# First half of k over SyncE in fp32, loads held until the transposes before them, and a product put behind two copies

## The chip, the core and the metric

The kernel runs on one core of a Trainium2 chip. A core has five engines that work side by side, each through its own instruction queue in order: TensorE for matrix products (PE in the profile; its weight loads are PEld), VectorE (DVE), ScalarE (ACT), GpSimd (POOL) and SyncE (SP). Data moves between the chip's memory and the core's on-chip memory by 16 DMA engines. SyncE, ScalarE and GpSimd can issue DMAs; a DMA that changes the type on the way (fp32 in memory, bf16 on chip) is issued from GpSimd in this kernel. TensorE writes its products to PSUM banks; the other engines take them from there.

The metric is the device time of one execution in microseconds. Before the change it is 317.12 us, the median of three runs (315.88 to 319.26).

## The reference

Attention with pooled keys and values, followed by a feed-forward block with the activation h·cos(h). Batch 8, 8 heads, 576 tokens, head size 64; k and v are averaged over groups of 8 tokens, so that each head attends to 72 pooled positions.

```python
B, H, S, D = q.shape                       # 8, 8, 576, 64, float32
k_p = k.reshape(B, H, S // 8, 8, D).mean(axis=3)
v_p = v.reshape(B, H, S // 8, 8, D).mean(axis=3)
scores = np.matmul(q, k_p.transpose(0, 1, 3, 2)) / np.sqrt(D)
attn = softmax(scores)                     # over the 72 pooled positions
a = np.matmul(attn, v_p)
x = a.transpose(0, 2, 1, 3).reshape(B * S, H * D)     # 4608 tokens x 512
h = x @ w_in                               # 4608 x 2048
out = (h * np.cos(h)) @ w_out              # 4608 x 512
```

## The kernel before

**Tiles and stages.** The 4608 tokens form nine tiles of 512. A tile `t` goes through an up phase and a down phase. In the up phase (`up_mm`, `up_g`), eight steps `fp` each make two 128-column chunks of h by eight matmuls into one of three two-bank buffers `banks[fp % 3]`; ScalarE takes the cosine (line 280), VectorE multiplies into `g_sb` (line 283). In the down phase, 64 matmuls (`down_mm`, line 286) accumulate four blocks of 128 tokens in two alternating buffers `obanks`; VectorE copies each finished block out (`down_out`, line 292) and SyncE stores it (line 296). Since 576 tokens of a batch are more than 512 of a tile, batch `b = t + 1` is being prepared while tile `t` runs, and a rest of 64 tokens of batch `t` is done in tile `t` as well.

**Attention inside the down phase.** A list `fill` holds pairs of a position and a piece of attention work. Before down matmul number `n`, all pieces with a position up to `n` are issued. `scores` (line 198, then an exponential on ScalarE, line 202) and `values` (line 224, then two logarithms, one exponential that forms the inverse, and two products on VectorE that write the next tile's input `xT`, lines 230 to 233) work on four units of a batch, here named `S_(n, bank)` and `V_(n, bank)`. They share the buffers `banks` with one another, so a unit must have left a bank before the next can enter it. In tile 0 the down matmuls run in an order that uses the four quarters of the down weights one after another, for two token blocks at a time: the copies of the first two blocks come after matmuls 27 and 31.

**Pooling k and v, transposing q and k.** Batches 0 and 1 are loaded in a layout with two rows of positions to a partition pair (`load_even`, line 85, GpSimd) and pooled on TensorE (`pool_k_mm`, line 154; `pool_v_mm`, line 162), q is transposed on TensorE (`q_transpose_mm`, lines 189 and 190). From batch 2 on, GpSimd loads k, q and v (lines 104 and 85, from `load_kv` and `load_even`) and pools by additions (`pool_add`, lines 138 to 145), k into `kpz` and v into `vz`. The transposes are then DMAs that SyncE issues in the up phase: q's after step 0 (`q_transpose`, line 181), k's after step 2 (`k_transpose`, line 168), into `qT` and `kz[b % 2]`.

**What orders the work.** The schedule is by hand: each engine takes its instructions in the order in which the program issues them, and waits only for semaphores. GpSimd's order from batch 2 on is loads of k, q, v, then k's additions, then v's, batch after batch; it goes on as soon as buffers are free (two each for `kv_st` and `q_b`), however far TensorE is. SyncE's order is the output stores of a tile, then the next tile's q transpose, then its k transpose. The program's order in a tile with `t > 0` is: up phase with the two transposes of batch `t + 1`, loads of batch `t + 2` (lines 445 to 449), down phase, additions of batch `t + 2` (lines 467 to 469).

**The head.** Ahead of tile 0 lies batch 0 (lines 310 to 398). TensorE runs ten warm-up matmuls, pools the first half of k (heads 0 to 3), runs two more warm-up matmuls, transposes the first half of q, and then computes scores; the second halves follow, then v. GpSimd issues, in this order, the first half of k (line 318), two small index tables, the first half of q (line 327), the second half of k, an identity matrix, the second half of q, v, and then the weights and batch 1. VectorE builds the 0/1 matrix `groups` that pools.

Of the kernel before, what the change touches and what calls it, by code (L numbers as in the profile page):

```python
# [9 lines left out]
FP32 = mybir.dt.float32  # L10
BF16 = mybir.dt.bfloat16
# [8 lines left out]
def kernel(  # L20
# [9 lines left out]
    nc = tc.nc  # L30
    B, H, S, D = q.shape
# [8 lines left out]
    ROW = S // 64  # L40
# [6 lines left out]
    REST = (SEG[2], (0, H))  # L47
# [5 lines left out]
    consts = ctx.enter_context(tc.tile_pool(name="consts", bufs=1))  # L53
# [10 lines left out]
    g_sb = wpool.tile([128, FFCH, TILE], BF16, name="g_sb")  # L64

    SpA = -(-Sp // 16) * 16
    kz = [wpool.tile([128, 2 * H, SpA], BF16, name=f"kz{i}") for i in range(2)]
# [5 lines left out]
    banks = [psum.tile([128, 2, 512], FP32, name=f"bank{i}") for i in range(3)]  # L73
# [5 lines left out]
    staged = {}  # L79

    def even_view(src, b, j0=0, j1=KCH):
        return src[b, 2 * j0:2 * j1].rearrange("(j a) (p t) d -> (a p) j (t d)", a=2, t=ROW)

    def load_even(dst, b, src, j0=0, j1=KCH):
        nc.gpsimd.dma_start(out=dst[:, j0:j1].rearrange("p j t d -> p j (t d)"), in_=even_view(src, b, j0, j1))

    def kv_tile():
        return kvst.tile([128, 2 * H * POOL * D], BF16, name="kv_st", tag="kv_st")
# [9 lines left out]
    def q_tile(b):  # L98
        staged["q", b] = qst.tile([128, KCH, ROW, D], BF16, name="q_b", tag="q_b")

    def load_kv(b, which, src):

        st = kv_tile()[:Sp].rearrange("p (i h t d) -> p i h t d", i=2, h=H, t=POOL)
        nc.gpsimd.dma_start(out=st[:, 0].rearrange("p h t d -> p h (t d)"),  # L104
                            in_=src[b].rearrange("h (p t) d -> p h (t d)", t=POOL))
        staged[which, b] = st

    def load_w_in(cg):
        nc.gpsimd.dma_start(
            out=w_in_sb[cg],  # L110
            in_=moe_w_in[:, cg * 512:(cg + 1) * 512].rearrange("(k p) f -> p k f", p=128))
# [8 lines left out]
    half = (slice(0, 64), slice(64, 128))  # L120
# [10 lines left out]
    def pool_add(b, which):  # L131

        st = staged.pop((which, b))
        x = st[:, 0]
        s = st[:, 1].rearrange("p h t d -> p (h t d)").bitcast(FP32).rearrange(
            "p (h t d) -> p h t d", h=H, t=POOL // 2)
        add = nc.gpsimd.tensor_tensor
        add(out=s, in0=x[:, :, 0:4, :], in1=x[:, :, 4:8, :], op=ADD)  # L138
        add(out=s[:, :, 0:2, :], in0=s[:, :, 0:2, :], in1=s[:, :, 2:4, :], op=ADD)  # L139
        if which == "k":  # L140
            for slot in (0, 3):
                add(out=kpz[b % 2][:Sp, :, slot, :], in0=s[:, :, 0, :], in1=s[:, :, 1, :], op=ADD)  # L142
        else:
            s = s.rearrange("p (j a) t d -> p j a t d", a=2)
            add(out=v_part(b), in0=s[..., 0, :], in1=s[..., 1, :], op=ADD)  # L145
# [12 lines left out]
    def pool_v_mm(b, pair):  # L158
        vb = staged["v", b]
        for t in range(ROW):  # L160
            for hp, rows in enumerate(half):
                nc.tensor.matmul(pair[:Sp, hp, 0:KCH * D], lhsT=groups[rows, t, :], rhs=vb[rows, :, t, :],  # L162
                                 start=(t == 0), stop=(t == ROW - 1))
        nc.vector.tensor_copy(out=v_part(b).rearrange("p j a d -> p a j d"),
                              in_=pair[:Sp, :, 0:KCH * D].rearrange("p a (j d) -> p a j d", j=KCH))
# [39 lines left out]
    def x_out(b, u, rows):  # L205
        (c0, n), (h0, nh) = u
        return xT[rows, h0 // 2:(h0 + nh) // 2, b * S + c0:b * S + c0 + n]

    def cols(x, u):
        n = u[0][1]  # L210
        return x[:, 0:n * u[1][1] // 2].rearrange("p (j n) -> p j n", n=n)
# [3 lines left out]
        inv = asb.tile([128, 512], FP32, name="inv", tag="inv", bufs=3)  # L215
        return lnc[:, 0:w], inv[:, 0:w]

    def values(b, u, pair):

        (c0, n), (h0, nh) = u  # L220
        ex = att.pop(("ex", b, u))
        for i in range(nh):
            pj, hp = divmod(h0 + i, 2)
            nc.tensor.matmul(pair[:, hp, (i // 2) * n:(i // 2 + 1) * n],  # L224
                             lhsT=vz[b % 2][:, pj, 2 * hp:2 * hp + 2, :].rearrange("p a d -> p (a d)"),
                             rhs=ex[:, i * n:(i + 1) * n])
        w = nh * n // 2
        lnc, inv = inverse_tile(w)
        for hp in range(2):
            nc.scalar.activation(out=lnc[half[1 - hp]], in_=pair[half[1 - hp], hp, 0:w], func=ACTF.Ln)  # L230
        nc.scalar.activation(out=inv, in_=lnc, func=ACTF.Exp, scale=-1.0)  # L231
        for hp in range(2):
            nc.vector.tensor_mul(out=x_out(b, u, half[hp]), in0=cols(pair[half[hp], hp, :], u),  # L233
                                 in1=cols(inv[half[1 - hp]], u))

    def sums_first(b, u, cs):

# [77 lines left out]

    kv_even_tiles(0)
    q_tile(0)
    load_even(staged["k", 0], 0, k, 0, 2)

    row_of = consts.tile([128, ROW], FP32, name="row_of")  # L320
    for rows in half:
# [2 lines left out]
    first_of = consts.tile([128, Sp], FP32, name="first_of")  # L324
    nc.gpsimd.iota(first_of, pattern=[[POOL, Sp]], base=0, channel_multiplier=0,
                   allow_small_or_imprecise_dtypes=True)
    load_even(staged["q", 0], 0, q, 0, 2)
    load_even(staged["k", 0], 0, k, 2, 4)
    identity = consts.tile([128, 128], BF16, name="identity")
    make_identity(nc, identity)  # L330
# [6 lines left out]
                            in1=first_of.unsqueeze(1).to_broadcast([128, ROW, Sp]), op=mybir.AluOpType.subtract)  # L337
# [3 lines left out]
    nc.vector.memset(vz[0], float(POOL))  # L341
    ones = consts.tile([128, D], BF16, name="ones")
    nc.vector.memset(ones, float(POOL))
    half_pi = consts.tile([128, 1], FP32, name="half_pi")
    nc.vector.memset(half_pi, math.pi / 2.0)

# [21 lines left out]
    us = BY_HEADS  # L368
# [31 lines left out]
    for t in range(NT):  # L400
        b = t + 1
        for fp in range(FFCH // 2):
            up_mm(t, fp, 2 if t == 0 and fp < 2 else 0)
            between = ()
            if t == 0:
                if fp == 4:
                    puts = pool_k_mm(1, obanks[0], 0, 2), pool_k_mm(1, obanks[1], 2, 4)
                elif fp in (5, 6):
                    g0 = 9 * (fp - 5)
                    puts = q_transpose_mm(1, obanks[0], g0, g0 + 5), q_transpose_mm(1, obanks[1], g0 + 5, g0 + 9)  # L410
                if fp in (4, 5, 6):
                    puts[0](vec)
                    between = ((puts[1], act),)
            up_g(t, fp, between)
            if 0 < t and b < B:
                if fp == 0:
                    q_transpose(b)
                elif fp == 2:
                    k_transpose(b)
        mms = [(ms, fc) for ms in range(4) for fc in range(FFCH)]  # L420
        if t == 0:
            mms = [(ms, fc) for hm in range(2) for cg in range(4) for ms in range(2 * hm, 2 * hm + 2)
                   for fc in range(4 * cg, 4 * cg + 4)]


        def S_(n, bank):
            return lambda: scores(b, us[n], banks[bank])

        def V_(n, bank):
            return lambda: values(b, us[n], banks[bank])  # L430

        fill = []
        if t < B:
            exp_tables()
            fill = [(1, lambda: scores(t, REST, banks[2])), (12, lambda: values(t, REST, banks[1]))]
        if t == 0:
            fill[1:] = [(2, S_(0, 0)), (4, lambda: pool_v_mm(1, banks[1])), (8, lambda: values(t, REST, banks[2])),
                        (8, S_(1, 0)), (8, V_(0, 1)), (14, S_(2, 2)), (16, V_(1, 0)), (22, S_(3, 1)), (32, V_(2, 2)),
                        (40, V_(3, 0))]
        elif b < B:  # L440
            us = BY_TOKENS
            fill[1:1] = [(5, S_(0, 0))]
            fill += [(15, S_(1, 2)), (18, V_(0, 0)), (25, S_(2, 2)), (28, V_(1, 1)), (35, S_(3, 2)), (38, V_(2, 0)),
                     (46, V_(3, 1))]
        if 0 < t and b + 1 < B:
            load_kv(b + 1, "k", k)
            q_tile(b + 1)
            load_even(staged["q", b + 1], b + 1, q)
            load_kv(b + 1, "v", v)
        fi = 0  # L450
        if t == NT - 1:
            mms = mms[:-FFCH]
        for n, (ms, fc) in enumerate(mms):
            while fi < len(fill) and fill[fi][0] <= n:
                fill[fi][1]()
                fi += 1
            down_mm(obanks[ms % 2], ms, fc)
            if fc == FFCH - 1:
                down_out(t, ms, obanks[ms % 2])
        if t < B:  # L460
            sin_tables()
        if t == 0:
            load_kv(2, "k", k)
            q_tile(2)
            load_even(staged["q", 2], 2, q)
            load_kv(2, "v", v)
        if b + 1 < B:
            pool_add(b + 1, "k")
            pool_add(b + 1, "v")
    last_chunk()  # L470
# [28 lines left out]
```

## Time and profile before

| What | us |
|---|---|
| median of three runs | 317.12 |
| the profiled execution | 318.08 |
| its span, first to last instruction | 316.3 |
| PE busy | 297.4 |
| ACT busy | 205.7 |
| DVE busy | 173.3 |
| POOL busy | 130.9 |
| mean granted clock of TensorE | 0.984 of full |

The profile is of one execution. Busy time is summed by engine; an engine that is idle and not the bottleneck costs nothing. PE's 94% of the span says that most of the kernel is bound by TensorE; what can be changed without changing the matmuls is the remainder, where PE waits or runs at a reduced clock. A row of the timeline gives start, length, engine, line, operation, what is written from what, the number of merged instructions, and in brackets the idle time before it with what ended it. SPq rows are instructions of SyncE's queue, and their length is the time until the queue goes on, not until the data has landed. The granted clock is TensorE's, 1.00 being full speed.

### The profile page before, as it was taken

Reading aid. Unit: us, or ns where it says so; the run is one execution under the profiler, and the core shown is the slowest. Engines: PE = TensorE matmul, PEld = TensorE weight load, DVE = VectorE, ACT = ScalarE, POOL = GpSimd, SP = SyncE. Lnnn points to the kernel's source line nnn. Section 1 sums busy time; section 2 is a strip of 40 time slices with the busy share of each in tenths; the row PEclk is TensorE's granted clock in tenths of the full one; section 3 lists DMA queues with packets and bytes.
Section 4 is the critical chain, followed back from the end, with each engine's and each line's share of the span. In section 5 each row is a group of like instructions: output and inputs, shape, how many; then the busy total and the mean of one; then the engine's idle time right before and its main releaser. Section 6 shows DMA issues by size and latency. Waiting matters only on the chain.

```text
span 316.3 us, 4555 instructions
## 1 busy us (share of the span) xinstructions
PE 297.4 (94%) x1766; PEld 154.0 (49%) x1798; DVE 173.3 (55%) x213; ACT 205.7 (65%) x254; POOL 130.9 (41%) x88
## 2 busy tenths in 40 slices
PE   7789899999999299999999999999999999999995
PEld 2555554445544155445544554455445544444444
DVE  6358635565656315575557555755575557515721
ACT  1587787369956359569956995699569956705500
POOL 8572018955982991993298329810000000000000
PEclk9799999999999879999999999999999999999999
DMA  6999998399349909960997099602470230041023
GB/s 91 195 207 207 206 205 166 83 157 161 74 68 183 158 2 151 221 103 3 152 212 108 1 157 217 101 2 48 101 101 0 51 85 0 2 99 33 0 62 74
DMA packets 47847, 33.60 MB, mean 106 GB/s; under 512 B 25937, under 2 KB 43345, under 8 KB 47825
## 3 DMA queue, kind: packets, MB, share of 16 engines
q0 software_dynamic: 20016, 18.36, 37.6%
q1 hardware_dynamic: 27648, 14.82, 24.1%
q8 instruction: 14, 0.23, 0.3%
q10 hardware_dynamic: 160, 0.13, 0.2%
q14 instruction: 9, 0.07, 0.1%
HBM read 36.70 MB, written 9.44 MB: 146 GB/s over the span
## 4 chain that ended last, share of the span: by engine, by line
PE 65%; DMA 15%; POOL 11%; ACT 2%; issue 1%; DVE 1%; POOLq 0%; ACTq 0%; DVEq 0%
PE obank L286 29%; PE bank L273 28%; DMA kv_st<-in_k_dram 12%; POOL kv_st L138 6%; PE bank L224 3%; PE bank L198 3%; POOL kv_st L139 3%; DMA kz<-kpz 2%; POOL kpz L142 2%; PE bank L304 1%; ACT ex L202 1%; ACT L261 0%; ACT cos L280 0%; PE obank L256 0%; POOL vz L145 0%
## 5 line engine op out<-in xcount | busy, mean ns | idle before, releaser
L286 PE MATMUL obank<-w_out_sb,g_sb 128*128 128x512 bf16 x542 | 133.1, 382 | 1.1 <-DVE o_sb L292 0.3
L273 PE MATMUL bank<-xT,w_in_sb 128*128 128x512 bf16 x563 | 125.5, 379 | 0.6
L280 ACT ACTIVATE cos<-bank,half_pi 128x1024 f32<-128x1024 f32 x72 | 80.2, 1115 | 67.3 <-PE bank L273 63.7
L283 DVE TENSOR_TENSOR g_sb<-bank,cos 128x1024 bf16<-128x1024 f32 x72 | 88.1, 1224 | 50.2 <-ACT cos L280 50.2
L273 PEld LDWEIGHTS <-w_in_sb 128*128 128x128 bf16 x576 | 56.1, 98 | 67.3 <-issue 0.4
L286 PEld LDWEIGHTS <-g_sb 128*128 128x128 bf16 x560 | 54.1, 98 | 52.1 <-issue 2.0
L233 DVE TENSOR_TENSOR xT<-bank,inv 64x512 bf16<-64x512 f32 (+1 forms) x72 | 45.3, 630 | 61.0 <-ACT inv L231 57.6
L138 POOL TENSOR_TENSOR kv_st<-kv_st 72x2048 f32<-72x2048 bf16 x12 | 48.8, 4064 | 39.7 <-DMA kv_st<-in_k_dram 39.7
L230 ACT ACTIVATE lnc<-bank 64x512 f32<-64x512 f32 (+1 forms) x72 | 39.2, 544 | 9.2 <-PE bank L224 7.3
L202 ACT ACTIVATE ex<-bank 72x1024 bf16<-72x1024 f32 (+1 forms) x40 | 36.2, 925 | 7.0 <-PE bank L198 6.9
L292 DVE COPY o_sb<-obank 128x512 f32<-128x512 f32 x35 | 23.5, 689 | 15.4 <-PE obank L286 14.8
L198 PE MATMUL bank<-qT,kz 128*72 128x256 bf16 (+1 forms) x192 | 23.8, 257 | 7.3 <-DMA kz<-kpz 6.4
L139 POOL TENSOR_TENSOR kv_st<-kv_st 72x1024 f32<-72x1024 f32 x12 | 28.2, 2347 | 1.0
L198 PEld LDWEIGHTS <-kz 128*72 128x72 bf16 x192 | 18.0, 119 | 16.5 <-DMA kz<-kpz 6.8
L231 ACT ACTIVATE inv<-lnc 128x512 f32<-128x512 f32 (+1 forms) x36 | 21.0, 582 | 1.1
L224 PE MATMUL bank<-ex,vz 72*128 72x256 bf16 (+1 forms) x176 | 20.1, 244 | 0.3 <-ACT ex L202 0.2
L224 PEld LDWEIGHTS <-vz 72*128 72x128 bf16 x176 | 14.0, 98 | 9.7 <-issue 1.1
L142 POOL TENSOR_TENSOR kpz<-kv_st 72x512 bf16<-72x512 f32 x12 | 15.0, 1267 | 0.5
L145 POOL TENSOR_TENSOR vz<-kv_st 72x512 bf16<-72x512 f32 x6 | 7.6, 1265 | 18.1 <-PE bank L224 17.9
L261 ACT ACT_TABLE_LOAD x9 | 11.5, 1283 | 0.9 <-PEq L483 0.7
L264 ACT ACT_TABLE_LOAD x9 | 11.5, 1283 | 0.2
L104 POOL DMA_DIRECT2D kv_st<-in_v_dram x6 | 5.0, 842 | 10.2 <-PE bank L162 10.2
(55 smaller groups left out, 86.8 us busy)
## 6 DMA issues: line engine op xcount, KB each, us to landing
out_dram<-o_sb SPq DMA_DIRECT2D x70, 128.0 KB, 2.5
kv_st<-in_v_dram POOLq DMA_DIRECT2D x8, 576.0 KB, 14.6
kv_st<-in_k_dram POOLq DMA_DIRECT2D x7, 576.0 KB, 9.0
q_b<-in_q_dram POOLq DMA_DIRECT2D x6, 576.0 KB, 11.5
w_in_sb<-in_moe_w_in_dram POOLq DMA_DIRECT2D x4, 512.0 KB, 13.7
w_out_sb<-in_moe_w_out_dram POOLq DMA_DIRECT2D x4, 512.0 KB, 18.3
q_b<-in_q_dram POOLq DMA_DIRECT2D x4, 288.0 KB, 12.2
kv_st<-in_k_dram POOLq DMA_DIRECT2D x2, 288.0 KB, 5.5
```

Source lines behind the costliest of these rows:

```text
L138: add(out=s, in0=x[:, :, 0:4, :], in1=x[:, :, 4:8, :], op=ADD)
L139: add(out=s[:, :, 0:2, :], in0=s[:, :, 0:2, :], in1=s[:, :, 2:4, :], op=ADD)
L198: nc.tensor.matmul(flat[:Sp, i * n:(i + 1) * n].rearrange("p (g n) -> p g n", n=64), lhsT=kz[b % 2][:, 2 * (h0 + i) + r, 0:Sp], rhs=att["q ...
L202: nc.scalar.activation(out=ex[:, 0:nh * n], in_=flat[:Sp, 0:nh * n], func=ACTF.Exp, scale=scale / POOL)
L224: nc.tensor.matmul(pair[:, hp, (i // 2) * n:(i // 2 + 1) * n], lhsT=vz[b % 2][:, pj, 2 * hp:2 * hp + 2, :].rearrange("p a d -> p (a d)"), ...
L230: nc.scalar.activation(out=lnc[half[1 - hp]], in_=pair[half[1 - hp], hp, 0:w], func=ACTF.Ln)
L233: nc.vector.tensor_mul(out=x_out(b, u, half[hp]), in0=cols(pair[half[hp], hp, :], u), in1=cols(inv[half[1 - hp]], u))
L273: nc.tensor.matmul(h[:, j, :], lhsT=w_in_sb[fc // 4][:, ki, (fc % 4) * 128:(fc % 4 + 1) * 128], rhs=xT[:, ki, t * TILE:(t + 1) * TILE], st ...
L280: nc.scalar.activation(out=cos, in_=h, func=ACTF.Sin, bias=half_pi[:, :1])
L283: nc.vector.tensor_mul(out=g_sb[:, 2 * fp:2 * fp + 2, :], in0=h, in1=cos)
L286: nc.tensor.matmul(o, lhsT=g_sb[:, fc, ms * 128:(ms + 1) * 128], rhs=w_out_sb[fc // 4][:, fc % 4, :], start=(fc == 0), stop=(fc == FFCH - 1))
L292: nc.vector.tensor_copy(out=o[:, 0:n], in_=ps)
```

## The change

Four edits, which the diff shows in this order.

The first half of k for batch 0 is no longer loaded and cast by a GpSimd DMA. SyncE loads it as fp32 into `g_sb`, which is free until tile 0 writes it, and ScalarE copies it to bf16 in k's tile. The first half of q takes the place of k as GpSimd's first load; it had stood behind the two index tables.

In tile 0 the pieces of attention work get other positions in the list `fill`. The pooling of v for batch 1 moves from 4 to 8, the second scores from 8 to 11, the first values from 8 to 13, the third scores from 14 to 18, the second values from 16 to 21, the fourth scores from 22 to 26.

The product that ends the second values is not issued with them but at position 32, that is, behind the copies of the first two output blocks on VectorE.

In tiles 1 to 5 the loads of batch `t + 2` move in the program from before the down phase to behind it, and a copy of one element of `kz[b % 2]` by GpSimd goes ahead of them. `kz[b % 2]` is written by the k transpose of batch `b = t + 1`, so GpSimd waits for that transpose before it issues the loads. In tile 0 the loads stay where they were and have no such copy.

```diff
+    def load_q(b):
+        q_tile(b)
+        load_even(staged["q", b], b, q)
+
...
-    def values(b, u, pair):
+    def values(b, u, pair, later=None):
...
         nc.scalar.activation(out=inv, in_=lnc, func=ACTF.Exp, scale=-1.0)
-        for hp in range(2):
-            nc.vector.tensor_mul(out=x_out(b, u, half[hp]), in0=cols(pair[half[hp], hp, :], u),
-                                 in1=cols(inv[half[1 - hp]], u))
+
+        def mul():
+            for hp in range(2):
+                nc.vector.tensor_mul(out=x_out(b, u, half[hp]), in0=cols(pair[half[hp], hp, :], u),
+                                     in1=cols(inv[half[1 - hp]], u))
+
+        if later is None:
+            mul()
+        else:
+            later.append(mul)
...
     kv_even_tiles(0)
     q_tile(0)
-    load_even(staged["k", 0], 0, k, 0, 2)
+    k_first = g_sb.rearrange("p f n -> p (f n)").bitcast(FP32)[:, 0:2 * ROW * D]
+    nc.sync.dma_start(out=k_first.rearrange("p (j n) -> p j n", j=2), in_=even_view(k, 0, 0, 2))
+    nc.scalar.copy(out=staged["k", 0][:, 0:2].rearrange("p j t d -> p (j t d)"), in_=k_first)
+    load_even(staged["q", 0], 0, q, 0, 2)
...
-    load_even(staged["q", 0], 0, q, 0, 2)
     load_even(staged["k", 0], 0, k, 2, 4)
...
+    gate = consts.tile([1, 1], BF16, name="gate")
...
-        def V_(n, bank):
-            return lambda: values(b, us[n], banks[bank])
+        later = []
+
+        def V_(n, bank, wait=None):
+            return lambda: values(b, us[n], banks[bank], wait)
...
         if t == 0:
-            fill[1:] = [(2, S_(0, 0)), (4, lambda: pool_v_mm(1, banks[1])), (8, lambda: values(t, REST, banks[2])),
-                        (8, S_(1, 0)), (8, V_(0, 1)), (14, S_(2, 2)), (16, V_(1, 0)), (22, S_(3, 1)), (32, V_(2, 2)),
-                        (40, V_(3, 0))]
+            fill[1:] = [(2, S_(0, 0)), (8, lambda: pool_v_mm(1, banks[1])), (8, lambda: values(t, REST, banks[2])),
+                        (11, S_(1, 0)), (13, V_(0, 1)), (18, S_(2, 2)), (21, V_(1, 0, later)), (26, S_(3, 1)),
+                        (32, lambda: later.pop()()), (32, V_(2, 2)), (40, V_(3, 0))]
...
-        if 0 < t and b + 1 < B:
-            load_kv(b + 1, "k", k)
-            q_tile(b + 1)
-            load_even(staged["q", b + 1], b + 1, q)
-            load_kv(b + 1, "v", v)
...
-        if t == 0:
-            load_kv(2, "k", k)
-            q_tile(2)
-            load_even(staged["q", 2], 2, q)
-            load_kv(2, "v", v)
+        if 0 < t and b + 1 < B:
+
+            nc.gpsimd.tensor_copy(out=gate, in_=kz[b % 2][0:1, 0, 0:1])
         if b + 1 < B:
+            load_kv(b + 1, "k", k)
+            load_q(b + 1)
+            load_kv(b + 1, "v", v)
             pool_add(b + 1, "k")
             pool_add(b + 1, "v")
```

## The prediction

> **What bounds the kernel now.** I read the windows first, with one window for each token tile (from the first up-projection matmul of the tile to that of the next), then the waits by engine, then the timeline of the tiles that stand out. The window rows give start:end and length, then busy us (instructions) of PE, PEld, DVE, ACT and POOL, the granted clock, the DMA share and GB/s.
>
> ```profile
> span 316.3 us, 4555 instructions
> 20.10:57.72 37.62, 35.47 (x281) 19.26 (x286) 22.21 (x30) 28.07 (x39) 15.47 (x13) 1.00 1.07 185
> 57.72:89.36 31.64, 31.48 (x174) 16.35 (x176) 18.57 (x23) 24.19 (x30) 24.63 (x12) 1.00 0.69 119
> 89.36:129.52 40.16, 33.59 (x174) 16.98 (x177) 18.83 (x23) 24.48 (x30) 26.46 (x16) 0.92 0.85 127
> 129.52:161.33 31.81, 31.65 (x175) 16.45 (x177) 18.99 (x23) 24.14 (x30) 19.65 (x12) 1.00 0.69 120
> 224.62:256.27 31.65, 31.44 (x173) 16.36 (x176) 18.82 (x23) 24.19 (x30) 0.00 (x0) 1.00 0.36 63
> ```
>
> Tiles 1 and 3 to 6 take 31.64 to 31.81 us (the first and last of the last four are shown), with PE busy nearly throughout: TensorE bounds them, and nothing in the change lowers its work. Three stretches stand out: the 20.1 us before tile 0, tile 0 with 37.62 us, and tile 2, which does the same work as tile 1 in 40.16 us at a mean clock of 0.92. Tile 2 therefore loses 40.16 - 31.65 = 8.5 us. Its timeline says why:
>
> ```profile
> 64.33 1.36 SPq L168 DMA_TRANSPOSE kz<-kpz  x1
> 65.27 0.86 POOL L104 DMA_DIRECT2D kv_st<-in_k_dram  x1
> 74.35 4.06 POOL L138 TENSOR_TENSOR kv_st<-kv_st 72x2048 f32<-72x2048 bf16 x1 [6.61 <-DMA kv_st<-in_k_dram]
> 80.91 2.49 POOL L142 TENSOR_TENSOR kpz<-kv_st 72x512 bf16<-72x512 f32 x2
> 91.15 0.84 POOL L104 DMA_DIRECT2D kv_st<-in_k_dram  x1
> 92.31 10.76 SPq L181 DMA_TRANSPOSE qT<-q_b  x1
> 103.16 5.37 SPq L168 DMA_TRANSPOSE kz<-kpz  x1
> 103.67 1.03 PE L286 MATMUL obank<-w_out_sb,g_sb 128*128 128x512 bf16 x4
> 111.05 1.07 PE L198 MATMUL bank<-qT,kz 128*72 128x256 bf16 x4 [6.35 <-DMA kz<-kpz]
> 132.41 3.18 SPq L181 DMA_TRANSPOSE qT<-q_b  x1
> ```
>
> GpSimd runs ahead of PE here. It starts the loads of batch 4 at 91.15, and 1.2 us later SyncE issues the q transpose of batch 3, which shares the DMA engines with the loads of a whole batch. The issue alone takes 10.76 us where the same instruction takes 3.18 us in tile 3. SyncE works in order, so the k transpose gets out only at 103.16, although its source was complete at 80.91 + 2.49 = 83.4, and PE waits 6.35 us for it.
>
> ```profile
> DMA to landing us min/median/max: 4.9/5.5/17.8
> kz<-kpz SPq DMA_TRANSPOSE x6, 3.9
> 112.00:114.00 2.00, 2.00 (x6) 0.66 (x5) 0.00 (x0) 1.02 (x1) 1.92 (x2) 0.50 0.03 8
> ```
>
> The first row belongs to the q transposes (line 181): 5.5 us to landing is usual, and this one is the 17.8. The last row shows the aftermath: the granted clock is 0.50 after the wait, so the matmuls that follow run at half speed. 6.35 us of wait and some 2.1 us of half clock make up the 8.5.
>
> **The gate and the later loads: -8.5 us.** For tiles 1 to 5 GpSimd first copies one element of kz, which k's DMA transpose writes, and only then issues loads for the next batch. Nothing else stands between on GpSimd's queue, so the three load issues and six additions pass no other instruction; they are queued behind the new wait, and SyncE's next transposes wait for them in turn. The copy itself is one element, five times, while GpSimd would idle anyway: nothing, and 0.1 to 0.3 us each if it were busy.
>
> In tile 1 the gate opens when kz of batch 2 has landed, 64.33 + 3.9 = 68.2, where loads went out at 65.27: 3 us later at most. By then no transpose is in flight until the next tile, so tile 2 finds the queues empty. Its q transpose goes out some 3 us after the tile's start (132.41 against 129.52 in tile 3), the k transpose 3.2 us after that, and kz lands 3.9 us later, about 10 us into the tile. Scores need it after the 64 up matmuls, five down matmuls and the last scores of the batch before, in tile 2 at 103.67 + 1.03 - 89.36 = 15.3 us. That leaves 5 us of slack, as in tiles 3 to 6, so I take the whole 8.5.
>
> The opposite cost is that the loads start later. From 65.27 to 74.35 k takes 9.1 us, and the additions to 83.4 another 9.0. A gate at 10.3 us of a tile gives kpz at 28.4; it is wanted at 31.65 + 6.2 = 37.8 in the next tile. So 9 us are to spare, and the cover fails only if the load and additions take 27 us instead of 18. I keep 0 for its cost, with the bounds 0 and the price in the rival below.
>
> **The head: -2.4 us.** Windows of 1 us, then the timeline:
>
> ```profile
> 1.00:2.00 1.00, 0.53 (x2) 0.26 (x3) 0.92 (x2) 1.00 (x1) 0.73 (x1) 1.00 0.00 0
> 1.27 0.87 POOL L85 DMA_DIRECT2D kv_st<-in_k_dram  x1 [0.82 <-POOLq L483]
> 2.79 0.76 POOL L85 DMA_DIRECT2D q_b<-in_q_dram  x1
> 5.85 0.77 PE L154 MATMUL obank<-groups,kv_st 64*64 64x72 bf16 x36
> 6.55 0.61 PE L365 MATMUL bank<-warm 128*128 128x512 bf16 x2
> 6.67 1.28 DVE L129 CAST kz<-obank 64x144 bf16<-64x144 f32 x4 [0.30 <-PE obank L154]
> 9.01 0.51 PE L189 MATMUL bank<-identity,q_b 128*128 128x128 bf16 x5 [1.85 <-DMA q_b<-in_q_dram]
> 11.70 1.93 ACT L202 ACTIVATE ex<-bank 72x1024 bf16<-72x1024 f32 x2 [1.12 <-PE bank L198]
> 20.21 0.63 ACT L247 ACTIVATE inv<-lnc 128x512 f32<-128x512 f32 x1
> 10.00:12.50 2.50, 2.33 (x11) 1.53 (x12) 0.06 (x1) 1.38 (x2) 1.12 (x2) 0.50 1.20 195
> out_dram<-o_sb SPq DMA_DIRECT2D x70, 128.0 KB, 2.5
> L280 ACT ACTIVATE cos<-bank,half_pi 128x1024 f32<-128x1024 f32 x72 | 80.2, 1115 | 67.3 <-PE bank L273 63.7
> ```
>
> k's first half is used at 5.85, when PE's opening warm-up ends as well, so an earlier k alone is worth nothing. In fp32 over SyncE it takes between 2.5 us (the 128 KB stores of that queue) and 4.6 us (GpSimd's load, 1.27 to 5.85), then a ScalarE copy of 128x1152, estimated from the 128x1024 row at 1.115 x 1152/1024 = 1.25 us. SyncE's first issue has no row; with 1.0 us, k is there at 4.8 to 6.9. I take the middle, 5.8, because the payload is nearest to GpSimd's load but the DMA engines are idle then (share 0.00): no change, ends -0.1 and +1.0.
>
> The gain is q's. Its half is issued at 1.27 in place of 2.79. It lands between 1.27 + 4.6 = 5.9 (as k did alone) and 1.27 + 6.2 = 7.5 (its present 2.79 to 9.01, behind another load); I take 6.6, since k still shares the engines, from another queue. PE has its warm-up done at 7.16, so the wait of 1.85 us goes. What is late next is the first copy of qT: five transposes take 0.51 us, to 7.67, and DVE is at its kz casts until 7.95; the second copy is on ScalarE, which is free, and the scores need both. So this is -1.9. The clock was 0.50 after that wait, from 10.0 to 12.5. PE works at that rate for most of the 1.7 us up to the first exponential at 11.70; at full rate I estimate another -0.5. From the first exponential at 11.70 to the last inverse at 20.84 ScalarE is nearly gapless, so the head moves as a block: -2.4, with ends -0.5 (late k) and -2.8.
>
> On the cause of that drop, the Trainium skill ("TensorE: Matmul & The Clock Gate", Part 1) says that the clock halves after an idle window of about 3.4 us. The 1.85 us here are shorter, so the trace does not agree in the head; by the rule the -0.5 would not come and the head would give -1.9.
>
> The other moves here are later issues on GpSimd, each earlier by the 0.8 us of the issue that left its queue. They feed a DMA stream that is full through most of tile 0 (the first row below). With the bf16 half of k no longer in it (128 x 1152 x 2 bytes = 295 KB), it runs ahead by 295 KB at 204 GB/s = 1.4 us.
>
> **Tile 0: -1.6 us.** The rate just used, the waits inside tile 0, and the loads of the down weights:
>
> ```profile
> 42.00:44.00 2.00, 1.76 (x12) 0.99 (x11) 0.84 (x2) 1.95 (x4) 0.00 (x0) 1.00 1.26 204
> 38.97 1.17 PE L162 MATMUL bank<-kv_st,groups 64*72 64x256 bf16 x18 [0.89 <-DVE g_sb L283]
> 43.54 0.63 PE L198 MATMUL bank<-qT,kz 128*72 128x256 bf16 x4 [0.24 <-ACT ex L202]
> 46.86 0.63 PE L198 MATMUL bank<-qT,kz 128*72 128x256 bf16 x4 [0.53 <-DVE xT L233]
> 50.37 1.89 PE L286 MATMUL obank<-w_out_sb,g_sb 128*128 128x512 bf16 x8 [0.29 <-DVE o_sb L292]
> 48.21 1.39 DVE L233 TENSOR_TENSOR xT<-bank,inv 64x512 bf16<-64x512 f32 x2 [1.40 <-ACT inv L231]
> L114 POOL DMA_DIRECT2D w_out_sb<-in_moe_w_out_dram x4: 740/744/757, 15.0 to 25.5; - x4
> DMA to landing us min/median/max: 17.0/18.3/18.6
> ```
>
> These four waits sum to 1.95 us. The new list puts four more down matmuls ahead of v's pooling (0.9 us, the first wait), three ahead of the second scores, and more between each scores and its values. The product at 48.21 stands ahead of the two output copies today and makes PE wait 0.29 for obank; behind them it does not. Played through by these durations, the order leaves about 0.15 for bank 1, 0.1 where the last scores meet the second product, and 0.15 where the last values meet the delayed one: 0.4 remain, so -1.6 (ends 0 and -1.95). All of this rides on the down weights: the last quarter lands about 25.5 + 18.3 = 43.8 today, 42.4 with the stream 1.4 ahead. It is wanted at down matmul 24, about 45.6 - 2.4 = 43.2, and the second quarter has some 0.4 us of margin by the same sum. The load of v for batch 2 waits for the pooling of v, which now ends at the same 40.1, less 2.4: no cost.
>
> **Sum.** -8.5 - 2.4 - 1.6 = -12.5 us. The profiled execution took 318.08 us (its span and 1.8 us around it), giving 305.6. It stands 0.96 above the median of 317.12, and from the median the sum is 304.6; I take 305.2.
>
> **Rivals.** *The head gains only issue time.* If the two first halves share the engines so that q lands hardly sooner, only the 0.8 us taken from GpSimd's queue comes: 318.08 - 8.5 - 1.6 - 0.8 = 307.2. For it: the DMA engines are full by 10.0 us (share 1.20), and k's load is on them together with q's. Against it: they stand idle before 2 us, time that SyncE's load can use. The Trainium skill ("DMA: Bandwidth & Descriptors", Issuing engines are not separate DMA queues) states this rule, that issuing from several engines saves only the issue time; the idle window above shows no engine saturated there.
>
> *The transposes stay slow.* If something other than loads, say the output stores ahead on SyncE, stretched the q transpose, tile 2 keeps its loss: 318.08 - 4.0 = 314.1. Against it: tile 3 has the same stores and needs 3.18 us.
>
> *The gate becomes the bound (slower).* Each load chain then runs from kz to kz: load, additions 9.0, transposes 3.2 + 3.9. With a load of 15.5 us it equals a tile of 31.65; above that every tile waits. The longest load of this line took 21.1 us:
>
> ```profile
> DMA to landing us min/median/max: 8.7/13.7/21.1
> ```
>
> The five gated batches would then add 5 x 5.6 = 28 us: 318.08 - 12.5 + 28 = 333.6. Against it: that load stood behind a full queue in tile 0; at 65.27 one took 9.1.
>
> **Chances.** Forecast 0.73, head by issue time 0.15, transposes slow 0.07, gate as bound 0.05. The range, 302.8 to 310.0, holds the first two with the bounds of head (late k, +1.9) and tile 0 (+1.6), and the median's 1 us below. About 1% (3.2 us) is what a measurement of this kernel can tell from no change. The third case lies at that edge, so: faster 0.90, within 0.05, slower 0.05.
>
> **What would show it.** Tile 2 at 31.7 us with a clock of 1.00 and a q transpose issue near 3 us; each k load issued just after kz lands; no wait of PE on q_b near 7 us and the first exponential near 9.3; tile 0 at 36 us with no wait on o_sb. I am wrong if a wait for kz or qT stands in tiles 3 to 6, if PE waits for w_out_sb in tile 0, or if k's cast ends after 7.

## The result, and the profile after

The kernel after takes 305.48 us, the median of four runs (305.23 to 305.81), against 317.5 us for the kernel before in the same comparison (315.88 to 319.26): a ratio of 0.9621 with a 95% interval of 0.9568 to 0.9675. The profiled execution took 305.34 us, with a span of 303.6. Single executions of the kernel before lie some microseconds apart, those of the kernel after within 0.6 us; what that has to do with the change is part of the experiments. The ratios leave out runs that are over 1.5% above the fastest of their kernel, which also show a lower granted clock.

The windows by tile, in the columns of the prediction (start:end and length, busy time of PE, PEld, DVE, ACT and POOL, clock, DMA share, GB/s):

```profile
17.63:53.56 35.93, 35.74 (x287) 19.34 (x286) 22.30 (x30) 28.18 (x39) 13.93 (x10) 1.00 1.17 203
53.56:85.21 31.65, 31.65 (x178) 16.35 (x177) 18.59 (x23) 24.19 (x30) 26.07 (x16) 1.00 0.65 121
85.21:116.86 31.65, 31.65 (x178) 16.33 (x177) 18.83 (x23) 24.19 (x30) 20.98 (x12) 1.00 0.64 119
```

Between the two profiled executions the spans differ by 316.3 - 303.6 = 12.7 us, and three places hold all of it: the head 20.10 - 17.63 = 2.5, tile 0 37.62 - 35.93 = 1.7, tile 2 40.16 - 31.65 = 8.5. In tile 2 PE is busy for all of its 31.65 us. The timeline of tile 2 shows the new order of SyncE and GpSimd, with PE's scores at the end:

```profile
88.14 2.00 SPq L185 DMA_TRANSPOSE qT<-q_b  x1
90.23 1.39 SPq L172 DMA_TRANSPOSE kz<-kpz  x1
93.86 0.18 POOL L475 COPY gate<-kz 1x1 bf16<-1x1 bf16 x1 [4.98 <-DMA kz<-kpz]
94.10 0.85 POOL L104 DMA_DIRECT2D kv_st<-in_k_dram  x1
100.37 0.60 PE L202 MATMUL bank<-qT,kz 128*72 128x256 bf16 x4
```

The q transpose is issued in 2.00 us where it took 10.76. The gate opens 8.65 us into the tile, the loads follow, and the scores come at 100.37 without a wait: kz is there 6.5 us ahead of them. The gate costs GpSimd waiting, as the sum of its waits says (25.9 us over four of them, the longest 7.4), but nobody pays for it: tiles 1 to 6 all take 31.64 or 31.65 us, and PE waits for kz in none of them.

```profile
POOL gate L475 <- DMA kz<-kpz: 25.9, 4, 7.4
```

In the head, the fp32 load by SyncE, its cast, and what PE and ScalarE do next:

```profile
4.22 1.15 ACT L331 CAST kv_st<-g_sb 128x1152 bf16<-128x1152 f32 x1 [2.19 <-DMA g_sb<-in_k_dram]
7.64 0.45 PE L193 MATMUL bank<-identity,q_b 128*128 128x128 bf16 x5 [0.90 <-DMA q_b<-in_q_dram]
9.41 1.93 ACT L206 ACTIVATE ex<-bank 72x1024 bf16<-72x1024 f32 x2 [0.47 <-PE bank L202]
47.52 4.06 POOL L142 TENSOR_TENSOR kv_st<-kv_st 72x2048 f32<-72x2048 bf16 x1 [8.71 <-DMA kv_st<-in_k_dram]
```

k's cast ends at 5.37. q's transposes still wait 0.90 us, to 7.64, and the first exponential begins at 9.41 in place of 11.70. The last row is GpSimd's first addition on the k of batch 2; it starts when that load has landed, and the load stands at the end of the first, full DMA stream.

### The profile page after: what moved, and what is told of

Its sections match the earlier page's. It is cut to its first block, busy times and chain, and to the rows that moved or that the text cites. A ratio compares the mean times of both kernels' runs of the same rounds, so it can differ in the third digit from the quotient of the medians.

```text
span 303.6 us, 4590 instructions
## 1 busy us (share of the span) xinstructions
PE 295.3 (97%) x1798; PEld 152.5 (50%) x1798; DVE 173.3 (57%) x213; ACT 206.6 (68%) x255; POOL 131.8 (43%) x92
## 4 chain that ended last, share of the span: by engine, by line
PE 85%; DMA 9%; POOL 3%; ACT 1%; issue 0%; DVE 0%; POOLq 0%; ACTq 0%
PE obank L297 38%; PE bank L284 36%; DMA w_out_sb<-in_moe_w_out_dram 6%; PE bank L228 5%; PE bank L202 4%; DMA w_in_sb<-in_moe_w_in_dram 3%; PE bank L315 1%; POOL kpz L372 1%; POOL kv_st L85 1%; POOL q_b L85 1%; ACT L272 0%; ACT cos L291 0%; POOL identity masks.py:199 0%; ACT ex L206 0%; DVE o_sb L303 0%
## 5 line engine op out<-in xcount | busy, mean ns | idle before, releaser
L202 PE MATMUL bank<-qT,kz 128*72 128x256 bf16 (+1 forms) x192 | 22.7, 248 | 0.3 <-ACT qT L194 0.2
L475 POOL COPY gate<-kz 1x1 bf16<-1x1 bf16 x5 | 0.9, 180 | 25.9 <-DMA kz<-kpz 25.9
L85 POOL DMA_DIRECT2D q_b<-in_q_dram x10 | 7.7, 773 | 2.9 <-DMA w_in_sb<-in_moe_w_in_dram 1.4
```

What stands on the lines that cost most here:

```text
L202: nc.tensor.matmul(flat[:Sp, i * n:(i + 1) * n].rearrange("p (g n) -> p g n", n=64), lhsT=kz[b % 2][:, 2 * (h0 + i) + r, 0:Sp], rhs=att["q ...
```

## The experiments

Each kernel is the kernel after with the edit shown, except e1, which is the kernel before with one. e1 to e4 share one chip and its runs of the kernel before, e5 to e8 the next, e9 to e12 the last.

**e1: the gate alone, in the kernel before.**

```diff
+        if 0 < t and b + 1 < B:
+            nc.gpsimd.tensor_copy(out=gate, in_=kz[b % 2][0:1, 0, 0:1])
         if b + 1 < B:
+            load_kv(b + 1, "k", k)      # and q, v; gone from ahead of the down phase
```

> The kernel before with the gate alone: loads of batch t + 2 behind the down phase and behind the copy of kz; head and tile 0 as before. Theory (the gate removes the meeting of loads and transposes in tile 2, 8.5 us): tile 2 in 31.7 us, q transpose issue near 2 to 3 us, time 308.0 to 309.5. Rival (something else slows the transposes, and the gain came from the shift of the head and tile 0): tile 2 stays above 36 us, time above 313.

Measured: 310.02 us (307.61 to 312.06), ratio to the kernel before 0.9771 (0.9681 to 0.9861). Against a difference of 2% the times alone leave it unclear. In the windows of the profiled execution (307.61 us), tile 0 is as before and tile 2 is whole:

```profile
18.14:55.75 37.61, 35.89 (x285) 19.26 (x285) 22.20 (x30) 27.96 (x38) 16.10 (x12) 1.00 1.13 195
87.40:119.05 31.65, 31.65 (x178) 16.35 (x177) 18.82 (x23) 24.18 (x30) 19.53 (x12) 1.00 0.64 119
```

The tile says plainly which theory holds: with the old head and the old tile 0, the gate alone makes tile 2 31.65 us instead of 40.16, which is 8.5 us. The times say less. The four runs fall into two pairs, 307.61 and 308.16 at a mean clock of 0.998 or more, 311.88 and 312.06 at 0.989. The median, 0.5 above the expected range, lies in the gap between them. Where the slower pair lost its clock is not shown, since neither run has a profile.

**e2: everything but the gate.**

```diff
-        if 0 < t and b + 1 < B:
-            nc.gpsimd.tensor_copy(out=gate, in_=kz[b % 2][0:1, 0, 0:1])
```

> The kernel after without the copy that gates the loads; all else as after. GpSimd then issues the loads of batch 4 when the additions for batch 3 end, near 88.9 us, and the q transpose of batch 3 goes out near 88.1. Theory A (what counts is whether load packets are in the queues while the transposes move): q's transpose gets out just ahead of the loads, k's meets them and lands near 98, wanted at 100.3: time 305.5 to 307. Theory B (without the gate the loads meet the transposes in tile 2 as before): a wait of 6 us on kz and half clock after it, time 313 to 314.5.

Measured: 313.46 and 314.47 us in the two runs that the ratio counts, 0.9874 of the kernel before (0.9786 to 0.9962, unclear against 2%); the other two took 321.3 us. The two counted runs lie 8.5 us above the 305.48 of the kernel after, so what the gate is worth is gone, and both lie where theory B put them. The timeline of tile 2 (profiled execution, 314.47 us):

```profile
88.38 2.78 SPq L185 DMA_TRANSPOSE qT<-q_b  x1
88.66 0.84 POOL L104 DMA_DIRECT2D kv_st<-in_k_dram  x1
91.25 5.01 SPq L172 DMA_TRANSPOSE kz<-kpz  x1
106.61 1.07 PE L202 MATMUL bank<-qT,kz 128*72 128x256 bf16 x4 [5.84 <-DMA kz<-kpz]
```

Theory A falls. The q transpose did go out ahead of the loads, by 0.28 us, and its issue took only 2.78 us; but the k transpose met the loads (5.01 us to issue), and PE waits 5.84 us. A head start of 0.28 us protects nothing here, where a q transpose usually takes 5.6 us to land. The place of the loads in the program does nothing either: without the copy they are in the same program order as in the kernel after. It is the wait that holds them. Theory B holds; what the two runs at 321.3 us met besides is not shown by any profile here.

**e3 and e6: the old head.** The same kernel on two chips; e5 is the kernel after beside e6.

```diff
-    nc.sync.dma_start(out=k_first.rearrange("p (j n) -> p j n", j=2), in_=even_view(k, 0, 0, 2))
-    nc.scalar.copy(out=staged["k", 0][:, 0:2].rearrange("p j t d -> p (j t d)"), in_=k_first)
-    load_even(staged["q", 0], 0, q, 0, 2)
+    load_even(staged["k", 0], 0, k, 0, 2)
...
+    load_even(staged["q", 0], 0, q, 0, 2)     # behind the two index tables, as before
```

> The kernel after with the head as before: first half of k by GpSimd first, first half of q behind the index tables. Theory: the head was worth 2.4 us (1.9 of waiting, 0.5 of clock), so 307.9, with the granted clock at 0.50 over 10.0 to 12.5 and the first exponential at 11.7. Rival (only the issue time of 0.8 us counts): 306.3.

> The kernel after once more, on the same chip as the three that follow, as their yardstick: 305.2 to 305.8.

> The kernel after with the head as before, again, for its spread: 305.85 to 311.57 in four runs, with mean granted clocks of 1.00, 1.00, 0.987 and 0.983. Theory (q's first half lands at a time that varies, and a PE idle for over a microsecond so early falls to half clock): again a spread of 3 us or more, each slow time with a clock below 0.99; median 307 to 309. Rival (the spread came from elsewhere on that chip): all within 1 us.

Measured: e3 305.85, 306.35 and 308.8 us in the three runs that the ratio counts, and 311.57 in a fourth; e5 305.30 (304.73 to 305.88), e6 306.15 (305.92 to 307.27). The middle one of e3's three runs is at the rival's 306.3. On the chip where e5 and e6 ran side by side the new head is worth 0.85 us, not 2.4. The timeline of e6:

```profile
7.95 0.45 PE L193 MATMUL bank<-identity,q_b 128*128 128x128 bf16 x5 [0.28 <-DMA q_b<-in_q_dram]
9.71 1.93 ACT L206 ACTIVATE ex<-bank 72x1024 bf16<-72x1024 f32 x2 [0.47 <-PE bank L202]
18.25 6.02 PE L284 MATMUL bank<-xT,w_in_sb 128*128 128x512 bf16 x26
```

With the old order q was there at 7.95, not at 9.01 as in the profiled execution before, the first exponential starts at 9.71, and tile 0 at 18.25. In the profiles of e3 and e1 the old order has q at 7.41 and 8.04. The same order of loads thus delivers q at times 1.6 us apart. And q is not all that tile 0 waits for, as e3 shows:

```profile
7.41 0.45 PE L193 MATMUL bank<-identity,q_b 128*128 128x128 bf16 x5 [0.73 <-DMA q_b<-in_q_dram]
14.37 1.17 PE L166 MATMUL bank<-kv_st,groups 64*72 64x256 bf16 x18 [0.79 <-DMA kv_st<-in_v_dram]
18.25 6.02 PE L284 MATMUL bank<-xT,w_in_sb 128*128 128x512 bf16 x27
```

Here q comes 0.23 us earlier than in the kernel after, whose transposes start at 7.64, and still tile 0 starts 0.62 us later than its 17.63, because PE waits 0.79 us for v. The spread that e6 was to repeat came back as 1.35 us only, with clocks of 0.997 and above, so its first theory, too, holds in part only: q's time varies, but how often it is late differed between the two calls.

**e7: the old head with more warm-up.**

```diff
-    warm_up(2, banks[1][:, 0, :])      # between pooling k and transposing q
+    warm_up(9, banks[1][:, 0, :])
```

> The same with nine warm-up matmuls in place of two between the pooling of k's first half and the transposes of q's, so that PE works until q is there (about 1.5 us more of them). They compute nothing that is used. Theory (the half clock is the larger part of what a late q costs): clocks 0.995 or above in every run, all runs within 1.5 us, median 306.3 to 307. Rival (the cost is the wait for q itself, or a later DMA): the spread of e6 stays.

Measured: 306.51 us (306.31 to 309.0). Five of the six runs lie within 0.65 us, but the one at 309.0 had a clock of 0.994, which the theory excluded; it has no profile. Since e6 beside it had little spread to remove, this run decides nothing; e9 and e10 put the late q there on purpose.

**e9 and e10: q late, without and with warm-up.** Both have the old head; k's second half is loaded ahead of q's first.

```diff
-    load_even(staged["q", 0], 0, q, 0, 2)
     load_even(staged["k", 0], 0, k, 2, 4)
+    load_even(staged["q", 0], 0, q, 0, 2)
...
-    warm_up(2, banks[1][:, 0, :])      # e10 only
+    warm_up(12, banks[1][:, 0, :])
```

> The kernel after with the old head, and q's first half moved behind k's second half on GpSimd, so that q lands about 1.5 us later than in e6 (9 to 9.5 in place of 7.4 to 8.0). Theory (a late q costs its wait and, once PE has been idle for some 2 us this early, a spell of half clock): clock 0.990 or less in most runs, time 308.5 to 312. Rival (a late q costs its wait alone): 307 to 308, clock 1.00.

> The same with twelve warm-up matmuls in place of two ahead of the transposes of q, so that PE is busy until q lands. Theory: the clock stays at 0.995 or above and the time at 307 to 308, that is, the wait alone. Rival (the idle PE has nothing to do with the clock): as e9.

Measured: e9 308.16 us (307.95 to 308.43), e10 307.31 (307.10 to 307.56). The timeline and a window of e9:

```profile
9.38 0.45 PE L193 MATMUL bank<-identity,q_b 128*128 128x128 bf16 x5 [1.95 <-DMA q_b<-in_q_dram]
10.73 1.91 PE L202 MATMUL bank<-qT,kz 128*72 128x256 bf16 x8
10.00:12.50 2.50, 2.28 (x11) 1.50 (x9) 0.36 (x1) 1.25 (x2) 1.38 (x2) 0.50 1.17 182
```

and the same of e10:

```profile
9.87 0.45 PE L193 MATMUL bank<-identity,q_b 128*128 128x128 bf16 x5 [0.93 <-DMA q_b<-in_q_dram]
10.91 1.13 PE L202 MATMUL bank<-qT,kz 128*72 128x256 bf16 x8
10.00:12.50 2.50, 2.50 (x51) 1.90 (x51) 0.49 (x1) 1.45 (x2) 0.97 (x2) 1.00 1.18 189
```

e9 is the head of the profiled execution before, made on purpose: a wait of 1.95 us, half clock over 10.0 to 12.5, and eight score matmuls in 1.91 us. In e10, q comes even later, at 9.87, yet PE's idle time is 0.93 us, the clock stays at 1.00 and the same eight matmuls take 1.13 us; the kernel is 0.85 us faster than e9. The whole-run clocks agree in all four runs of each, 0.992 to 0.994 in e9 and 0.998 to 1.00 in e10, though e9 stops short of the figures of its theory (0.990 or less, 308.5 us or more). So the half clock that the prediction set for a late q is real, and filling most of the wait with matmuls removes it, at 0.85 us. For the wait alone there is only 307.31 - 306.15 = 1.2 us between e10 and e6, from two chips, which is no more than a hint.

**e4 and e11: the old positions, and the new ones without the delayed product.** e4 has the list of the kernel before. e11:

```diff
-                        (11, S_(1, 0)), (13, V_(0, 1)), (18, S_(2, 2)), (21, V_(1, 0, later)), (26, S_(3, 1)),
-                        (32, lambda: later.pop()()), (32, V_(2, 2)), (40, V_(3, 0))]
+                        (11, S_(1, 0)), (13, V_(0, 1)), (18, S_(2, 2)), (21, V_(1, 0)), (26, S_(3, 1)),
+                        (32, V_(2, 2)), (40, V_(3, 0))]
```

> The kernel after with the old positions of the attention pieces in tile 0 and no delayed product. Theory: the order was worth 1.6 to 1.7 us, by waits of PE for bank 1, the exponential, the product and the output copy: 307.1, tile 0 in 37.6 us. Rival (tile 0 is held by the arrival of the down weights, so the order gives little): 305.5 to 306.

> The kernel after with the product issued with its values, ahead of the two output copies; the other new positions stay. Theory: the product at position 21 is then done before the copies are due, because its inverse is ready about 46.3 us and the copy of block 0 only waits for the rest of the product: at most 0.3 us of PE waiting, 305.3 to 305.7. Rival (the delayed product is what the new order rests on): 306 or more.

Measured: e4 306.98 us (306.82 to 307.13), 1.5 above the 305.48 of the kernel after; e11 306.35 (306.20 to 306.48), 0.9 above it; the three stem from different comparisons. In the profiles tile 0 takes 37.61 us in e4 (from 17.60 to 55.21), 36.80 in e11 (from 17.88 to 54.68) and 35.93 in the kernel after. The timeline of e11:

```profile
45.17 1.39 DVE L239 TENSOR_TENSOR xT<-bank,inv 64x512 bf16<-64x512 f32 x2 [1.40 <-ACT inv L235]
46.59 1.29 DVE L303 COPY o_sb<-obank 128x512 f32<-128x512 f32 x2
47.34 1.89 PE L297 MATMUL obank<-w_out_sb,g_sb 128*128 128x512 bf16 x8 [1.15 <-DVE o_sb L303]
```

My theory for e11 falls, and its rival holds. VectorE starts the product at 45.17, since its inverse is ready only then, and is at it until 46.56; block 0 is finished meanwhile, its copy starts at 46.59, and PE waits 1.15 us for the buffer. In the kernel after no such wait is left:

```profile
43.80 0.63 PE L202 MATMUL bank<-qT,kz 128*72 128x256 bf16 x4
46.00 1.89 PE L297 MATMUL obank<-w_out_sb,g_sb 128*128 128x512 bf16 x8
44.90 0.69 DVE L303 COPY o_sb<-obank 128x512 f32<-128x512 f32 x1 [1.15 <-PE obank L297]
46.48 1.39 DVE L239 TENSOR_TENSOR xT<-bank,inv 64x512 bf16<-64x512 f32 x2
```

Of the 1.7 us that the edit takes from tile 0, 0.9 hang on the delayed product: by themselves the new positions bring the output copies nearer to the product and give 0.8.

**e12: the loads late.**

```diff
+            for _ in range(8):
+                nc.gpsimd.memset(idle, 0.0)      # behind the gate, ahead of the loads
```

> The kernel after with eight fills of an unused tile by GpSimd (1.8 us each, 14.3 us in all) between the gate and the loads. They compute nothing that is used. The rival in which the gate becomes the bound, made real: GpSimd's own loop is then 14.3 + 0.3 gate + 7.6 load + 9.0 + 7.7 additions = 39 us against a tile of 31.65. Theory (9 us of slack at most, counted to k's transpose; 7 us counted over GpSimd's whole loop): tiles 1 and 2 still 31.65 us, tiles 3 to 6 longer by 6 to 9 us each, total 328 to 342. Rival (loads have all the time of a tile): 305 to 307.

Measured: 344.39 us, one run. Two of the gates, one row of the fills, the waits of PE for kz in sum, the first of them, and one more wait of PE, in the head:

```profile
104.92 0.18 POOL L476 COPY gate<-kz 1x1 bf16<-1x1 bf16 x1
105.04 14.80 POOL L478 MEMSET idle<- 80x2048 bf16 x8
145.04 0.18 POOL L476 COPY gate<-kz 1x1 bf16<-1x1 bf16 x1
PE bank L202 <- DMA kz<-kpz: 26.7, 4, 7.4
140.76 1.07 PE L202 MATMUL bank<-qT,kz 128*72 128x256 bf16 x4 [7.39 <-DMA kz<-kpz]
PE bank L166 <- DMA kv_st<-in_v_dram: 1.6, 1, 1.6
```

The gate is now the bound, as the slower rival described: GpSimd's loop takes 145.04 - 104.92 = 40.1 us, and four tiles wait for kz, 26.7 us together. The first gated batch is absorbed by the slack: tiles 1 and 2 take 31.65 us, and tiles 3 to 6 take 40.86 to 41.75. The other 12 us of the 39 are not waits for kz. One part lies in the head, where PE waits 1.6 us for v in this execution. The rest lies in the same four tiles: the four matmuls after each wait take 1.07 us, as in tile 2 of the kernel before, where 0.60 is usual (100.37 above), and the granted clock is 0.50 in the 3.4 to 4.2 us after each of the four waits. Each of these tiles is thus 9.2 to 10.1 us longer, where I had 6 to 9, and the total lies 2 us above my range.

**e8: q's first half over SyncE as well.**

```diff
-    load_even(staged["q", 0], 0, q, 0, 2)
+    q_first = g_sb.rearrange("p f n -> p (f n)").bitcast(FP32)[:, 2 * ROW * D:4 * ROW * D]
+    nc.sync.dma_start(out=q_first.rearrange("p (j n) -> p j n", j=2), in_=even_view(q, 0, 0, 2))
+    nc.scalar.copy(out=staged["q", 0][:, 0:2].rearrange("p j t d -> p (j t d)"), in_=q_first)
```

> The kernel after with q's first half also over SyncE in fp32, into the part of g_sb behind k's, and cast by ScalarE after k's cast. PE waited 0.90 us for q in the kernel after. Theory: q lands by 5.5, its cast ends near 6.6, transposes near 6.8 to 7.0, the DMA stream of GpSimd is another 0.5 us or so earlier: 0.5 to 0.9 us faster than e5. Rival (two fp32 loads share the engines, k lands later and holds the pooling): no gain, 0 to +1 us.

Measured: 304.53 us (304.47 to 305.26) beside 305.30 for the kernel after on the same chip. Against the kernel before the ratios are 0.9583 (0.9541 to 0.9624) and 0.9600 (0.9558 to 0.9642); the intervals overlap and so do the single runs, so the 0.8 us between the medians is near the limit of what the times can tell. The timeline shows where it comes from:

```profile
5.83 1.15 ACT L334 CAST q_b<-g_sb 128x1152 bf16<-128x1152 f32 x1 [0.24 <-DMA g_sb<-in_q_dram]
7.03 0.45 PE L193 MATMUL bank<-identity,q_b 128*128 128x128 bf16 x5
8.94 1.93 ACT L206 ACTIVATE ex<-bank 72x1024 bf16<-72x1024 f32 x2 [0.61 <-PE bank L202]
```

As the theory had it, q's transposes start at 7.03 without a wait; in e5 they start at 7.55, there too without one. The first exponential begins at 8.94, against 9.41 in the kernel after and 9.67 in e5, and tile 0 starts at 17.17, against 17.63 and 17.90. It is the fastest kernel measured here.

## Why the prediction was right, and where it was not

The forecast of 305.2 us against 305.48 came from the right places, and two of its three terms are confirmed by experiment. The third, the head, came out right between the two profiled executions and is too large in general.

*The gate, -8.5.* Right in mechanism and size: e1's tile 2 is 31.65 us instead of 40.16, and the kernel after loses 8.5 us in the two counted runs of e2, which lacks the gate alone. The rival that something other than loads slows the transposes is excluded by e1 and e2 together, in which the stores are the same and the gate alone decides. Its price was set at nothing, and that held; but the slack was mis-sized. I counted 9 us up to the k transpose. GpSimd must also finish v's additions before it comes to the next gate. In the kernel after it runs from the gate at 93.86 to the end of these additions at 118.7:

```profile
117.47 1.26 POOL L149 TENSOR_TENSOR vz<-kv_st 72x512 bf16<-72x512 f32 x1
```

That is 24.9 us of a tile of 31.65, so 6.8 us are to spare. e12's 14.8 us of fills make it 39.7, close to the 40.1 measured.

*The head, -2.4.* This is the step that failed. The profiles agree with it (2.5 us between the two executions), but e6 against e5 gives 0.85. I took the size from one execution, in which q had landed at 9.01; e3, e6 and e1 have it at 7.41 to 8.04 by the same order, with no half clock. What I described is what a late q costs, as e9 and e10 show, not what the old order costs in general.

The reason lies in the transfer of q, which I let land at 6.6 with no wait. In the profiles of the kernel after, e2, e4, e5, e11 and e12, q's load takes 6.1 to 6.3 us from issue to landing, so that it lands at 7.4 to 7.6. In the old order it is issued 1.5 us later and takes 4.6 us in e3, 5.1 in e6, 5.2 in e1, 5.4 in e7 and 6.2 in the kernel before. Most of the earlier issue is therefore lost to a longer transfer, as the rival "the head gains only issue time" had supposed; that k's load beside it is the reason is argued, not tested. What the new order does show is that q lands at nearly the same time in every profile.

But the rival's size, 0.8 us, is near the measured 0.85 by luck, since the issue time did not come. The identity matrix and the load of v, first before the change and then after it:

```profile
4.56 0.29 POOL masks.py:199 TENSOR_SCALAR_AFFINE_SELECT identity<-identity 128x128 bf16<-128x128 bf16 x1
5.52 0.78 POOL L85 DMA_DIRECT2D kv_st<-in_v_dram  x1
3.84 0.89 POOL masks.py:199 TENSOR_SCALAR_AFFINE_SELECT identity<-identity 128x128 bf16<-128x128 bf16 x1
5.38 0.78 POOL L85 DMA_DIRECT2D kv_st<-in_v_dram  x1
```

The instruction that makes the identity matrix takes 0.6 us more after the change, and v is issued only 0.14 us earlier; the prediction had 0.8 for all these issues. Why it takes longer is not shown. PE waits for v in e3 (0.79 us), e6 (0.25) and, with the new head, e11 (0.3) and e12 (1.6), but not in the kernel after and e5, so v's landing varies as q's does. How the 0.85 divides between q and v stays open.

Even between the two profiled executions, the term holds two errors that cancel. q's transposes start 9.01 - 7.64 = 1.37 us earlier, where I had 1.9. From there to the first exponential it takes 1.77 us in place of 2.69, so the full clock and what goes with it give 0.92, where I had 0.5.

k's cast was about right (5.37 for 5.8), and so, nearly, was the claim that k itself decides nothing: PE waits 0.20 us for the cast. The DMA stream runs ahead by less than I had: the k load of batch 2 has landed at 47.52. Before, this row read

```profile
48.45 4.06 POOL L138 TENSOR_TENSOR kv_st<-kv_st 72x2048 f32<-72x2048 bf16 x1 [7.18 <-DMA kv_st<-in_k_dram]
```

so it is 0.9 us and not 1.4.

*Tile 0, -1.6.* Right: 1.7 between the profiles, of the kernel before as of e4, and 1.5 by e4's median. In the kernel after PE never waits for the down weights. Of the part that I gave least weight, the product behind the copies (0.29 us of waiting in the old order), e11 shows that it matters more than that in the new one.

*The sum.* Taken singly the three give 8.5 + 0.85 + 1.5 = 10.9 us, and the medians differ by 12.0. The remaining 1.1 us can't be assigned with certainty, but the granted clocks suggest where to look. Of the 22 counted runs of the kernel before beside e1 to e12, twelve have a mean clock of 0.989 and take 316.9 us on average, seven have 0.983 or 0.984 and take 318.2, and three have less and take 320.3. The profiled execution is one of the 0.984 kind, with half clock in the head and in tile 2. All 24 runs of the kernel after, e4, e5, e8 and e11, which have both the new head and the gate, are at 0.997 or above. So a part of the 1.1 us may be how often the kernel before meets a late q; the runs without a profile don't show it.

The forecast came out near although the head's term is too large in general, because that term was taken from the same execution as the time from which it was subtracted: 318.08 holds the late q, 318.08 - 12.5 = 305.6 does not, and the kernel after has none.

The rule of the Trainium skill on the clock ("TensorE: Matmul & The Clock Gate", Part 1: idle for about 3.4 us) is not borne out in the head: an idle time of 1.95 us was enough in e9, and filling most of it kept the clock at 1.00 in e10. The rule of the Trainium skill in "DMA: Bandwidth & Descriptors" (Issuing engines are not separate DMA queues), that issuing from several engines saves only issue time, stands behind the rival. The 0.8 us worked out for the rival came nearer than my sum, but v's issue moved by 0.14 us only, and e8 gains another 0.8 us by the same means.

## What to carry to other kernels

An engine that runs ahead issues its loads whenever its buffers come free; if another queue has a short transfer on the critical path, look for the stage where the two meet, and hold the loads with a wait on that transfer, since moving them in the program does nothing when no other instruction stands between. Count the slack of such a wait around the whole loop of the engine that waits, everything up to its next wait included. And a term read from one execution is a term of that execution: where a transfer's landing decides it, ask for a second profile of the same order before setting its size. An earlier issue is not yet an earlier landing: here q was issued 1.5 us earlier, beside k's load, and against all profiles of the old order but one it landed less than a microsecond earlier.

## What the runs showed of the hardware that was not expected

A q transpose that was issued 0.28 us ahead of a load was not safe from it. In e2 the longest q transpose took 10.1 us to land (usual 5.6):

```profile
DMA to landing us min/median/max: 4.7/5.6/10.1
```

The clock of TensorE fell to half after 1.95 us of idle time at 9 us into the kernel, while idle times of 0.28 us (e6), 0.93 us (e10) and, at 8 us, 1.29 us left it at 1.00. The last is e1:

```profile
8.04 0.45 PE L189 MATMUL bank<-identity,q_b 128*128 128x128 bf16 x5 [1.29 <-DMA q_b<-in_q_dram]
```

And an fp32 load over SyncE with a cast on ScalarE had k's half ready at 5.37 us, the cast of 128x1152 taking 1.15 us.
